# Backward dO projection as column-tile passes, and doubled Q/K row tiles in the forward stage, of a recurrent transformer kernel

One NeuronCore of a Trainium2 chip (trn2) runs the whole program. The metric is device time in microseconds (us) of one execution. Every ratio below is the mean time of one kernel's fast runs over the mean of the other kernel's fast runs of the same rounds, so it is not quite the ratio of the medians that are quoted. Runs were on several chips, and the kernel before took 3682 to 3695 us (medians) on them; compare ratios across groups of runs, not microseconds.

## The reference

```python
for s in range(n_seg):                       # 64 segments of 32 rows, 8 memory rows in front
    h = concatenate([mem, xs], axis=1)       # 40 rows x 512
    q, k, v = (einsum('btd,dhe->bhte', h, W) for W in (Wq, Wk, Wv))   # 32 heads of 128
    p = softmax(where(mask, q @ k.T * scale, -1e9))
    o = einsum('bhte,hed->btd', p @ v, Wo)
    mem = o[:, :M]; outs.append(o[:, M:])    # the memory makes the segments a chain
# around it: layer norm with modulation, a gated linear unit; out: y and all gradients (vjp)
```

In the backward stage the segments run in reverse. For each one dO of every head is `Wo^T dy`. From it come dS, dV, dK, dQ, then `dh`, whose memory rows are the next segment's `dy`.

## The kernel before

The stages run one after the other: forward recurrence, GLU forward and backward, backward recurrence, weight gradients. A scheduler orders each engine's instructions when the program is built; GpSimd (POOL), VectorE (DVE), ScalarE (ACT) and the SP queue then work through theirs in that fixed order.

Backward stage, the projection and what follows it:

```python
rxp = tile_pool(name="p4rx", bufs=3)                    # row buffers for the transposed gradients
def get_dy(s):                                          # dy of a segment by DMA
    nc.sync.dma_start(t[:, :, M:L], self.DAOT[s])
def dot_bank(hb, eng):                                  # WoT stationary, dy (40 columns) moving
    for hh in range(nh):
        for c in range(DC):
            nc.tensor.matmul(ps[:, g_, hl*L:(hl+1)*L], lhsT=WoT[:, c, h*E:(h+1)*E], rhs=dyT[:, c, :], ...)
    self.evac(eng, part3(dOT, hb)[:, :, 0:120], ps[:, :, 0:120])
def grad_part(nm, lh, rh, xt, pi, eng):                 # ... at the end of dVT, dKT, dQT each:
    rows = rxp.tile([128, G, 128], BF16, name="rows_x")
    nc.sync.dma_start(rows[:], xt[:, :], transpose=True)               # SP: transpose, 352 KB
    nc.gpsimd.dma_start({"dVT": self.DVR, "dKT": self.DKR, "dQT": self.DQR}[nm][s], rows[:])   # store
```

Forward stage, what the argument touches:

```python
RA = {x: ptiles("RA" + x, 1, ...)[0] for x in "vkq"}    # one tile of projected rows for v, k, q
def p1_tile(j):                                         # layer norm of 128 rows, some tiles ahead
    x0 = p1w.tile([128, D], BF16, name="x0_1", bufs=1)
    nc.sync.dma_start(x0[:], x_rows[j*128:(j+1)*128, :])
    nc.vector.bn_stats(st[:], x0[:])
    # ... xh, h1 on VectorE, then transposes into hx
```

## Time and profile before

| | us |
|---|---|
| median of 4 runs | 3694.68 (3689.59 to 3696.75) |
| forward recurrence (98 to 1292) | 1194 |
| GLU and its gradients (1292 to 1937) | 645 |
| backward recurrence (1937 to 3044) | 1107 |
| weight gradients (3044 to 3695) | 651 |

In the two recurrences TensorE (PE) is busy over 90% of the time and the other engines feed it; what counts is whatever makes it wait. The prediction shows and reads the lines for this.

### The profile page before, as it was taken

To read this page: it belongs to the slowest core of one execution; us is meant where nothing else is said; L and a number is where in the kernel's file an instruction comes from. 1 tells how busy PE (TensorE), PEld (TensorE's weight loads), DVE (VectorE), ACT (ScalarE), POOL (GpSimd) and SP (SyncE) were. 2 spreads that over 40 slices of the span, in tenths; PEclk is the share of its full clock that TensorE was granted. 3 is DMA by queue.
4 is the path that set the end of the run, shared out by engine and by line. 5 is a ranking of instruction groups with operands and counts; after the bars stand their busy time and mean duration, and the time that the engine had idled before them with its cause. 6 is when DMAs were issued, how large, how long until landed. Compare 5 with 4: busy or idle time off the path is not lost.

```text
span 3696.3 us, 108208 instructions
## 1 busy us (share of the span) xinstructions
PE 3282.3 (89%) x45566; PEld 1897.6 (51%) x45566; DVE 1640.8 (44%) x4087; ACT 1208.9 (33%) x2742; POOL 957.9 (26%) x1917
## 2 busy tenths in 40 slices
PE   1889888899999969996989999999999994999996
PEld 1445444455555535553546666666666662445453
DVE  2454444455545556663225445444455541222222
ACT  0444444444544444442123333333333330000001
POOL 3333333333333323331111112111221221222221
PEclk6999999999999989998999999999999997999998
DMA  7565656566666653324779999999999998787774
GB/s 235 122 134 127 137 131 131 138 137 141 143 139 148 144 163 123 121 102 151 231 213 236 230 228 228 226 223 217 238 246 233 235 212 201 206 207 196 200 197 149
DMA packets 809259, 667.20 MB, mean 181 GB/s; under 512 B 511082, under 2 KB 683898, under 8 KB 808644
## 3 DMA queue, kind: packets, MB, share of 16 engines
q1 hardware_dynamic: 718948, 501.39, 60.5%
q0 software_dynamic: 31024, 103.06, 9.0%
q10 hardware_dynamic: 58800, 55.84, 5.8%
q8 instruction: 357, 5.85, 0.7%
q14 instruction: 130, 1.06, 0.1%
HBM read 292.82 MB, written 275.02 MB: 154 GB/s over the span
## 4 chain that ended last, share of the span: by engine, by line
PE 53%; DMA 5%; issue 3%; DVE 3%; ACT 1%; SPq 1%; POOL 0%; DVEq 0%; ACTq 0%; POOLq 0%
PE gps L1372 11%; PE dh_ps L208 10%; PE proj_ps L1138 6%; PE g_ps L1171 4%; PE gps5o L1382 3%; PE gps L941 3%; PE mm L855 3%; PE dh_tps L208 2%; PE tps L1103 2%; DMA Kst<-KST 2%; PE mm L788 1%; PE mm L792 1%; PE dp_ps L1161 1%; PE dp_ps L1157 1%; PE pass_ps L435 1%
## 5 line engine op out<-in xcount | busy, mean ns | idle before, releaser
L1372 PE MATMUL gps<-rows,hrows 128*128 128x512 bf16 (+2 forms) x2160 | 417.1, 355 | 0.0
L1372 PEld LDWEIGHTS <-hrows 128*128 128x128 bf16 x2160 | 211.4, 98 | 204.2
L647 POOL TENSOR_TENSOR Pst<-Pst,rden 120x1408 bf16<-120x1408 bf16 x64 | 162.7, 2542 | 415.4 <-DMA Pst<-ET 347.3
L1138 PE MATMUL proj_ps<-dyT,WoT 128*128 128x40 bf16 x8192 | 233.1, 180 | 19.4 <-issue 11.8
L1138 PEld LDWEIGHTS <-WoT 128*128 128x128 bf16 x8192 | 223.6, 96 | 30.6 <-issue 30.4
L63 DVE CAST ot<-gps 128x512 bf16<-128x512 f32 (+3 forms) x77 | 48.9, 635 | 395.2 <-PE gps L1372 259.7
L435 PEld LDWEIGHTS <-hT 128*32 128x32 bf16 x6144 | 140.5, 97 | 156.9 <-ACT hT L638 22.4
L234 DVE TENSOR_TENSOR dh_lo<-dh_ps,dh_hi 128x256 bf16<-128x256 f32 x128 | 48.4, 420 | 344.0 <-ACT dh_hi L230 344.0
L1382 PE MATMUL gps5o<-dyrows,rows 128*128 128x512 bf16 x640 | 141.4, 383 | 45.4 <-DMA rows<-OSR 45.4
L61 ACT ACTIVATE ot<-gps 128x512 bf16<-128x512 f32 (+3 forms) x77 | 42.4, 551 | 418.1 <-PE gps L1372 262.5
L208 PE MATMUL at_ps<-Wo,OT 128*32 128x512 bf16 x2048 | 135.0, 384 | 27.9 <-ACT OT L61 25.4
L61 ACT ACTIVATE dVT<-g_ps 128x512 bf16<-128x512 f32 (+1 forms) x192 | 107.8, 561 | 157.3 <-PE g_ps L1171 119.2
L208 PE MATMUL dh_ps<-WvT,dVT 128*32 128x512 bf16 x2048 | 151.8, 391 | 4.6 <-issue 4.5
L1376 POOL DMA_DIRECT2D out_dram<-ot x108 | 81.2, 752 | 281.9 <-DVE ot L63 153.5
L61 ACT ACTIVATE dOT<-proj_ps 128x480 bf16<-128x480 f32 (+2 forms) x192 | 68.4, 391 | 257.8 <-PE proj_ps L1138 250.5
L61 ACT ACTIVATE dQT<-g_ps 128x512 bf16<-128x512 f32 (+1 forms) x192 | 107.8, 561 | 125.1 <-PE g_ps L1171 125.1
L63 DVE CAST dKT<-g_ps 128x512 bf16<-128x512 f32 (+1 forms) x192 | 123.7, 644 | 44.0 <-PE g_ps L1171 43.2
L63 DVE CAST RAq<-pass_ps 128x512 bf16<-128x512 f32 x128 | 88.4, 691 | 121.8 <-PE pass_ps L435 121.8
L234 DVE TENSOR_TENSOR at_lo<-at_ps,at_hi 128x256 bf16<-128x256 f32 x128 | 48.4, 420 | 211.9 <-ACT at_hi L230 211.9
L61 ACT ACTIVATE OT<-tps 128x512 bf16<-128x512 bf16 (+1 forms) x192 | 101.0, 560 | 122.5 <-PE tps L559 91.1
L208 PE MATMUL dh_ps<-WkT,dKT 128*32 128x512 bf16 x2048 | 136.7, 388 | 0.0
L435 PE MATMUL pass_ps<-Wv,hT 128*32 128x512 bf16 x2048 | 126.8, 391 | 9.4 <-ACT hT L638 9.4
(364 smaller groups left out, 7230.7 us busy)
## 6 DMA issues: line engine op xcount, KB each, us to landing
OSR<-Ost SPq DMA_DIRECT2D x64, 352.0 KB
OT<-OT SPq DMA_DIRECT2D x64, 352.0 KB
PS<-Pst SPq DMA_DIRECT2D x64, 352.0 KB
OT_l<-OT SPq DMA_DIRECT2D x64, 352.0 KB
Pst_l<-PS SPq DMA_DIRECT2D x64, 352.0 KB
DVR<-rows_x POOLq DMA_DIRECT2D x64, 352.0 KB, 5.0
DKR<-rows_x POOLq DMA_DIRECT2D x64, 352.0 KB, 6.4
DQR<-rows_x POOLq DMA_DIRECT2D x64, 352.0 KB, 4.7
```

The costliest lines, as they stand in the source:

```text
L61: return nc.scalar.activation(out, in_, AF.Copy)
L63: return nc.vector.tensor_copy(out, in_)
L208: self.nc.tensor.matmul(ps[32 * j:32 * j + 32, :], lhsT=lhsT, rhs=w, start=(n < 4), stop=(n >= total - 4), tile_position=(0, 32 * j))
L234: nc.vector.tensor_tensor(lo[:], ps[:, 256 * h:256 * h + 256], parts[h][:], op=ALU.subtract)
L435: nc.tensor.matmul(ps[32 * j:32 * j + 32, :], lhsT=lhs(c), rhs=rhs, start=(c == 0), stop=(c == DC - 1), tile_position=(0, 32 * j))
L647: nc.gpsimd.tensor_tensor(Pst[0:120, :, :], Pst[0:120, :, :], rden[:, :].unsqueeze(2).to_broadcast([120, G, 128]), op=ALU.mult)
L855: nc.tensor.matmul(hp[:], lhsT=xT[:, fc, :], rhs=wT[:, fc, :], start=(n == 0), stop=(n == 2 * FC - 1))
L941: nc.tensor.matmul(ps[:], lhsT=h2r[:, j, c * 128:(c + 1) * 128], rhs=xr[:, j, :], start=(j == 0), stop=(j == NT - 1))
L1138: nc.tensor.matmul(ps[:, g_, hl * L:(hl + 1) * L], lhsT=WoT[:, c, h * E:(h + 1) * E], rhs=dyT[:, c, :], start=(c == 0), stop=(c == DC - 1))
L1171: nc.tensor.matmul(ps[:, j, :], lhsT=lh[:, g * GW:(g + 1) * GW], rhs=rh[:, g * GW:(g + 1) * GW], start=True, stop=True)
L1372: nc.tensor.matmul(ps[:, 0:ng * E], lhsT=hrows[:, tp_, c * 128:(c + 1) * 128], rhs=rows[:, tp_, 0:ng * E], start=(tp_ == 0), stop=(tp_ == ...
L1382: nc.tensor.matmul(ps[:], lhsT=rows[:, tp_, gg * E:(gg + 1) * E], rhs=dyrows[:, tp_, :], start=(tp_ == 0), stop=(tp_ == NTP - 1))
```

## The change

Intent of the backward part: let WoT be the moving operand, 512 columns at a time, with 32 columns of dy stationary, four column tiles side by side; 32 such matmuls take the place of 128 matmuls of 40 columns. The result lands in rows (RAd) and is turned by 8 transposes. The last 8 rows of each segment ("tails") don't fit into 32; they are projected for four segments together, one tile of four ahead (RBd), turned into `btd`, and copied into dOT by GpSimd. To make room the row buffers go from three to two. Intent of the forward part: K and Q rows in two tiles in turn, so that a store of rows doesn't hold the next segment's rows.

```diff
-            rxp = tile_pool(name="p4rx", bufs=3)
+            rxp = tile_pool(name="p4rx", bufs=2)
+            dOT, RAd, RBd, btd = ...                       # cut
+            def get_da(t):                                 # dy of four segments, one load
+                nc.sync.dma_start(d..., self.DAOT[4*t:4*t+4]...)
+                nc.gpsimd.tensor_copy(b..., d[:, :, :, 24:T])            # dyb, the tails
+            def proj_b(t, hf): self.col_pass(psp, WoT, hf, <dyb>, RBd, ("act", "dve")[hf])
+            def turn_b():
+                for hf in range(2):
+                    tp = self.turn_half(psp, RBd, hf)
+                    self.evac(("act", "dve")[hf], btd[:, 4*hf:4*hf+4, :], tp[:])
-                dot_bank(0, "act"); self.pop_later(); dot_bank(1, "dve"); ...
+                for hf in range(2):
+                    self.col_pass(psp, WoT, hf, lambda c: dyT[:, c, :], RAd, ("act", "dve")[hf])
+                to_heads("pool", btd[:], 0, 8, 32, 8, 8 * s4)          # two copies, btd -> dOT
+                for hf in range(2):
+                    tp = self.turn_half(psp, RAd, hf)
+                    to_heads(("act", "dve")[hf], tp[:], 4 * hf, 4, 0, 32, 0)
+                    prod(hf)
+                if s4 == 0:                                 # end of the body, s4 = s % 4
+                    if s > 0: turn_b()
+                elif s4 < 3 and s > 3: proj_b(s // 4 - 1, 2 - s4)
 # forward
-            RA = {x: ...}
+            RAs = [...]; RA = RAs[s % 2]                    # k and q doubled
-                if norms: norms.pop()()                     # now two steps later
-                outproj(0) ... outproj(1); outproj(2)
+                outproj(0, 6) ... outproj(6, 12) ... outproj(12, 24); outproj(24, H)
# fewer buffers: h1 2 -> 1, hx 5 -> 4, hb 4 -> 3 (cut)
# backward: work of the dh tails in eight pieces and not four; dyT copied by GpSimd out of get_da's tile (cut)
```

## The prediction

> **What bounds the kernel now.** I read the stages first (busy time of each engine in each stretch), then the waits of TensorE in the two recurrent stages, then the chain of work and the timelines of GpSimd and VectorE inside single segments. The change touches two stages: the forward recurrence (98 to 1292 us) and the backward recurrence (1937 to 3044 us), 64 segments each.
>
> ```profile
> 98.00:1292.00 1194.00, 1082.38 (x16922) 596.62 (x16920) 594.92 (x1804) 561.15 (x1468) 390.79 (x1050) 0.97 0.62 137
> 1937.00:3044.00 1107.00, 1047.89 (x21385) 698.12 (x21381) 545.98 (x1332) 347.58 (x795) 222.19 (x461) 0.98 1.07 230
> ```
>
> The columns are stretch, length, then busy time of PE, PEld, DVE, ACT, POOL. PE is busy 95% of the backward stage, so there it is matmul issue time that counts; one segment takes 1107 / 64 = 17.3 us, and one without a stall 16.1 to 16.5 us. The rest is waits:
>
> ```profile
> PE proj_ps L1138 <- issue: 11.8, 8, 2.8
> PE g_ps L1171 <- DMA Kst<-KST: 9.5, 7, 2.5
> ...
> PE dp_ps L1157 <- issue: 5.8, 3, 2.5
> ```
>
> All waits called "issue" in that stage sum to 30.7 us (11.8 + 5.8 + 4.5 + 3.4 + 3.2 + 2.0); in the forward stage they are 0.7 us. What waits there are is this:
>
> ```profile
> PE turn_ps L442 <- DVE RAq L63: 39.9, 8, 5.8
> PE at_ps L208 <- ACT OT L61: 24.3, 50, 0.8
> ...
> 266.66 0.69 DVE L302 BATCH_NORM_STATS2 st<-x 128x6 f32<-128x512 bf16 x1 [7.16 <-DMA x<-in_A_x_dram]
> ```
>
> The first line looks like a full row buffer RAq, which the doubled row tiles would cure. The VectorE timeline shows otherwise: VectorE stands for 7.16 us at the statistics of a later row tile, whose load the SP queue issued late (behind the store of P), and RAq's eviction is the next in its queue. It recurs each 78.6 us. No wait of TensorE or of an eviction for the stores of the K and Q rows shows up.
>
> **What the Trainium skill says.** (1) "TensorEngine Tiling", Key Properties: changing the tiling mode drains TensorE. The trace agrees: from a 128x32 column matmul to a 128x128 one the starts lie 312 ns apart, where the next column group would have followed after 206; back again it is 149 instead of 56 ns. (2) "TensorE: Matmul & The Clock Gate", Part 3, The mechanism: matmuls in different column tiles start about 4 ns apart and run together. The trace has 3 to 4 ns between the four and some 213 ns per group of four. (3) "Advanced Engine Details and Errata", ISA Cache: an instruction line is 16 KB, 256 instructions. The instruction queue moved 167 packets and 2.74 MB in the backward stage, 16.4 KB each, so I read the "issue" stalls as late instruction lines. (4) "DMA: Bandwidth & Descriptors", Issuing engines are not separate DMA queues: transfers from SP and GpSimd interleave on the same 16 engines, so store and transpose times below stretch when loads run beside them.
>
> **The change part by part, backward.** The projection of dO is now 128 matmuls of 40 columns:
>
> ```profile
> 2519.95 1.31 PE proj_ps L1138 x48
> ...
> 2521.32 1.19 PE proj_ps L1138 x48
> ...
> 2523.26 0.80 PE proj_ps L1138 x32
> ```
>
> That is 3.3 us of the path (25 ns apart, 128 x 0.025 = 3.2). After it there are 32 column matmuls, 8 groups x 0.213 = 1.7 us, 8 transposes x 0.056 = 0.45 us, and per four segments the same once more for the tails: (1.7 + 0.45) / 4 = 0.54 us. Bare sum 2.7 us, saving 0.6 us of PE time a segment, or 38 us. But PE work isn't what follows: the result lands in rows and has to be turned. In order, from the start of the passes: last pass matmul 1.5 us, its end 1.9, VectorE eviction (0.69 for 512 columns) 2.6, transposes 2.85, while ACT spreads the first half until 2.95; there the transposes of dOT can begin. VectorE then does the first product (0.42), a copy of 0.2 and the second half's spread (0.5), so its queue frees the second quarter's work at 4.4 us. In the kernel before, the same point (second group of transposes) came at 2524.05 - 2519.95 = 4.1 us. So the body of a segment becomes about 0.3 us longer, although 12 to 24 tail matmuls are now interleaved, because four mode switches (0.1 us each) and the longer evict, turn, spread chain eat the saving: 64 x 0.3 = +19 us.
>
> What is gained: PE instructions fall from 91134 to 81150 rows, and the burst of 256 rows in 3.3 us goes. The issue rate is then like the forward stage's (37 rows a us), which stalls 0.7 us in all: about -25 us. Kst is now loaded ahead of the dQT transpose on the SP queue: about -9 us (its wait).
>
> The expected loss is a new wait on GpSimd. The last 8 rows of each segment come from btd and are copied into dOT by GpSimd. For three segments of four the built program places these copies in the middle of the segment before. For the first of each tile of four (btd has only just been turned) they stand behind the store DQR of the segment before, which itself waits for the DMA transpose of dQT:
>
> ```profile
> 2524.26 0.54 POOL L1177 DMA_DIRECT2D DQR<-rows_x  x1 [3.70 <-DMA rows_x<-dQT]
> ...
> 2507.22 0.54 POOL L1177 DMA_DIRECT2D DQR<-rows_x  x1 [7.82 <-DMA rows_x<-dQT]
> ```
>
> Those are 4.3 and 7.5 us after the start of their segments (2519.95 and 2499.69); over all segments the median is 6.2, the range 3.4 to 10.8 (and the last one). The pool for these rows drops from three buffers to two, so the dQT transpose also waits until DVR has left its buffer (DVR is issued 4.4 to 6.5 us after its transpose and lands about 5 us later), some 1 to 3 us into the next segment; the transpose then lands 4.5 to 5.5 us later. I take 6.5 us. Then 0.54 for the issue and 0.6 for two copies: dOT complete at 7.65 instead of 2.95, a stall of 4.7 us in 15 segments, +70 us. Start of the stage (two passes and a turn of the first tails): +3 us.
>
> **Forward.** The order of instructions on GpSimd and SP in the steady state is the same in both built programs: moving the normalisation in the source doesn't move it. The doubled rows remove no wait that the trace has. Fewer buffers for hx shift one statistics instruction from the crowded start to the steady place, where each costs 5.4 us: +5 us. Splitting the output projection into 6, 6, 12, 8 heads lets ACT evict earlier, but adds two mode switches and one filler matmul ahead of the third part; both ways the last projection matmul starts 2.7 us after the first: 0. The sum: +19 - 25 - 9 + 70 + 3 + 5 = +63 us, 3757 us. I place the centre a little lower, at 3745, because the stall could be shorter where few loads run.
>
> **Rivals.** (a) The projection saving holds. If VectorE's queue is no limit after all and the copies come early (DQR at 4 us), the stall shrinks to 15 x 2.2 = 33 us and the body is 0.3 us shorter: 33 - 19 - 25 - 9 + 8 = -12, about 3680. For it speaks that PE is 95% busy; against it the fixed place of the copies in GpSimd's queue. (b) The two buffers become a ring that binds. A transpose plus a store takes 10 to 12 us of a buffer, three a segment over two buffers make 15 to 18 us, the length of a segment. If latencies don't fall, SP stands still at the transposes, and the loads of Qst and Kst come late in every segment: another 0.5 to 2 us x 64, so 3790 to 3870. Against it: the DMA engines have idle stretches in every segment, and a transpose alone moves its packets in 2 to 3 us. (c) The forward stage gains: if the doubled rows and the earlier evictions take the 5.4 us stalls away, -38 us. I see nothing that would.
>
> **Range and chances.** The stall is 33 to 120 us, the body -19 to +25, stalls removed -34 to -10, the forward stage -15 to +10. Together some 8 times in 10 between 3680 and 3805. Slower by over 2% begins at 3767.6, a little above my sum; faster by over 2% is 3619.9, which needs everything but the stall to turn out twice as well. So 0.03 faster, 0.66 within, 0.31 slower.
>
> **What would show it.** Right: in the waits of TensorE of the backward stage a line of 15 or so waits of 2 to 8 us of the transposes of dOT (or their products) for GpSimd's dOT copies, once per four segments; "issue" in that stage under 10 us; no Kst wait over a few us; the forward stage within 15 us of 1194 with its 5.4 us stalls intact, eight of them. Wrong: no such GpSimd wait (then the copies stood earlier, and the kernel is as fast or faster), waits for Qst, Kst or OT_l in most segments (rival b), or segments without a wait well under 16 us (rival a, my VectorE chain was too long).

## The result and the profile after

The changed kernel takes 3795.2 us (median of 4, 3788.76 to 3812.35); ratio 1.0281 (95% interval 1.0245 to 1.0318): slower. The profiled run, 3810.5 us, is the slowest of the four, so its sums are some 15 us on the large side.

Busy time of each engine in the two stages (columns as in the prediction: stretch, length, PE, PEld, DVE, ACT, POOL, then granted clock, DMA share, GB/s):

```profile
98.00:1296.00 1198.00, 1087.14 (x16906) 632.99 (x16897) 602.82 (x1805) 570.59 (x1470) 393.26 (x1043) 0.97 0.62 136
...
1942.00:3146.00 1204.00, 1068.08 (x16289) 610.37 (x16293) 576.41 (x1486) 372.46 (x821) 271.17 (x662) 0.95 0.90 209
```

The forward stage is 1198 us for 1194. The backward stage is 1204 for 1107, and its granted clock has fallen from 0.98 to 0.95. Waits of TensorE in it (us in total, times, longest):

```profile
PE tps L1150 <- POOL dOT L65: 98.2, 15, 10.1
PE g_ps L1211 <- DMA Qst<-QST: 12.7, 4, 4.5
PE dh_ft L261 <- ACT dh_hi L248: 8.9, 19, 0.5
```

There is the foretold wait, 15 times, once in four segments (in 14 of them the copies stand behind the store DQR; in the first, of 2.1 us, ahead of it). The 30.7 us named "issue" and the 9.5 us for Kst are gone; a wait for Qst is new. One of the 15, on three engines. First GpSimd's timeline, then that of the SP queue (SPq), then TensorE's (start, length, engine, line, instruction; in brackets the idle time before it and what ended it):

```profile
2399.56 0.54 POOL L1217 DMA_DIRECT2D DKR<-rows_x  x1 [4.39 <-DMA rows_x<-dKT]
2405.66 0.54 POOL L1217 DMA_DIRECT2D DQR<-rows_x  x1 [5.56 <-DMA rows_x<-dQT]
2406.20 0.53 POOL L65 COPY dOT<-btd 128x192 bf16<-128x192 bf16 x2
```

```profile
2397.40 0.38 SPq L1156 DMA_DIRECT2D Kst<-KST  x1
2399.34 1.38 SPq L1216 DMA_TRANSPOSE rows_x<-dQT  x1
2407.15 0.39 SPq L1101 DMA_DIRECT2D daq<-DAOT  x1
```

```profile
2398.80 0.39 PE L226 MATMUL turn_ps<-ident,RAd 128*128 128x128 bf16 x4
2406.61 0.50 PE L1150 MATMUL tps<-ident,dOT 128*128 128x128 bf16 x3 [7.43 <-POOL dOT L65]
...
2408.52 0.63 PE L1150 MATMUL tps<-ident,dOT 128*128 128x128 bf16 x4
2408.94 0.63 PE L1197 MATMUL dp_ps<-VT_l,dOT 128*128 128x128 bf16 x4
...
2412.04 0.39 PE L1211 MATMUL g_ps<-Pst_l,dOst 128*128 128x128 bf16 x4
```

The segment starts at 2395.59. The two copies stand in GpSimd's queue behind the store DQR, that store behind the transpose of dQT, and SP issues that transpose only at 2399.34, 1.6 us after the last load before it: it waits for a row buffer. The SP queue's waits in this stage put a name to it:

```profile
SPq L1216 <- DMA DVR<-rows_x: 199.7, 62, 5.1
```

In 62 segments the dQT transpose waited for the dV rows to leave their buffer. TensorE's lines show something the prediction left out: a group of four 128x128 matmuls takes 0.63 us after the stall and 0.39 us from 2412.04 on; the starts lie 0.42 and not 0.23 us apart. For 5.4 us TensorE runs at about half rate. The granted clock of two stretches says the same:

```profile
2393.20:2411.80 18.60, 10.24 (x129) 7.04 (x122) 7.21 (x20) 3.75 (x10) 3.97 (x10) 0.73 0.70 163
2411.80:2428.40 16.60, 16.60 (x263) 8.97 (x261) 7.64 (x22) 5.29 (x12) 2.31 (x5) 0.99 0.93 186
```

The Trainium skill has this in "TensorE: Matmul & The Clock Gate", Part 1: after an idle window of some 3.4 us the clock drops to half, and it comes back after about as long of steady work. The trace agrees: in this stage each of the 16 stalls of 3.4 us or more was followed by a slow stretch, of 2.9 to 6.3 us (TensorE's work at half clock, by the granted-clock records: the trace holds when the clock was granted at half, and the views show the mean). Of the three stalls between 1 and 3 us one was. A stall of 3.4 us isn't needed, though: in the stage of the kernel before (first profile) there is none over 2.9 us, and TensorE worked 33 us of it at half clock.

### The profile page after: what moved, and what is told of

Same layout as the page of the kernel before. It is cut to its first block, busy times and chain, and to the rows that moved or that the text cites. A ratio compares the mean times of both kernels' runs of the same rounds, so it can differ in the third digit from the quotient of the medians.

```text
span 3810.5 us, 98572 instructions
## 1 busy us (share of the span) xinstructions
PE 3311.5 (87%) x40498; PEld 1850.7 (49%) x40574; DVE 1680.1 (44%) x4247; ACT 1245.8 (33%) x2774; POOL 1018.7 (27%) x2128
## 5 line engine op out<-in xcount | busy, mean ns | idle before, releaser
L219 PEld LDWEIGHTS <-hT 128*32 128x32 bf16 x6144 | 163.3, 96 | 127.1 <-ACT hT L649 16.6
L208 PE MATMUL at_ps<-Wo,OT 128*32 128x512 bf16 x2048 | 171.9, 386 | 23.7 <-ACT OT L61 23.7
L1150 PE MATMUL tps<-ident,dOT 128*128 128x128 bf16 x704 | 90.4, 238 | 101.4 <-POOL dOT L65 98.2
L1217 POOL DMA_DIRECT2D DQR<-rows_x x64 | 34.7, 542 | 420.2 <-PE g_ps L1211 182.9
L219 PE MATMUL pass_ps<-Wk,hT 128*32 128x512 bf16 x2048 | 136.5, 383 | 0.0
L219 PE MATMUL pass_ps<-Wq,hT 128*32 128x512 bf16 x2048 | 134.0, 382 | 0.0
L582 DVE TENSOR_TENSOR Ost<-or_ps,rden 120x512 bf16<-120x512 f32 (+1 forms) x192 | 124.2, 647 | 19.2 <-PE or_ps L580 1.1
```

The costliest lines, as they stand in the source:

```text
L208: self.nc.tensor.matmul(ps[32 * j:32 * j + 32, :], lhsT=lhsT, rhs=w, start=(n < 4), stop=(n >= total - 4), tile_position=(0, 32 * j))
L219: self.nc.tensor.matmul(ps[32 * j:32 * j + 32, :], lhsT=lhs(c), rhs=rhs, start=(c == 0), stop=(c == DC - 1), tile_position=(0, 32 * j))
L582: nc.vector.tensor_tensor(part3(Ost, pi)[0:120, 0:n, :], or_ps[0:120, 0:n, :], rden[:, pi * PG:pi * PG + n].unsqueeze(2).to_broadcast([120 ...
L1150: nc.tensor.transpose(ps[:, j, :], src[:, g * w:g * w + GW], self.ident[:, :])
```

## The experiments

Twelve kernels ran, all with correct results, in three groups of four, each group on one chip. The kernel before ran beside each group: medians 3683.0, 3681.8 and 3689.2 us. What was expected of the first four in microseconds starts from the 3694.7 and 3795.2 us of the first measurement; there the ratio counts.

**1. Tails turned earlier (e1_turn_early).**

```diff
                 dstt(0)
+                if s4 == 0 and s > 0:
+                    turn_b()
                 grad_part("dVT", dOst, Pst, dVT, 1, "act")
 ...
                 if s4 == 0:
                     tail.begin(s, [WvT, WkT, WqT])
-                    if s > 0:
-                        turn_b()
```

> The changed kernel with one edit: the eight transposes that turn the tails of the next four segments stand in the middle of the fourth segment and not at its end, so the built program places GpSimd's two copies into dOT in the middle of that segment too, ahead of the transposed row stores. Theory A (the loss is these copies standing behind the store of the dQ rows, plus TensorE running at half rate for some 5 us after each such stall): TensorE's 98 us of waits for GpSimd's dOT copies fall to under 5, the slow stretch after each (18.45 us segments against 16.5) goes as well, about 25 us more, so 3795 - 98 - 25 = 3672, 3660 to 3690. Theory B (the ring of two row buffers is what binds, the copies only show it): TensorE then waits elsewhere, for Qst, Kst or OT_l in most segments, and the time stays above 3740.

Measured: 3754.8 us, ratio 1.0183 (1.015 to 1.0216). Neither theory holds alone. In the built program the copies stand ahead of the store, and the dOT wait is gone, but TensorE now waits here:

```profile
PE g_ps L1211 <- DMA Qst<-QST: 55.7, 21, 6.7
```

and SP's waits for the row buffers have grown in sum (DQR 95.8 and DVR 199.7 us in the changed kernel):

```profile
SPq L1216 <- DMA DQR<-rows_x: 186.7, 45, 9.0
SPq L1216 <- DMA DVR<-rows_x: 152.3, 55, 5.0
```

The stall of one engine had given another its slack. With the copies out of the way the ring of two buffers binds: the SP queue stands at the transposes, and the loads of Qst behind them come late.

**2. Three row buffers (e2_three_row_buffers).**

```diff
-            rxp = tile_pool(name="p4rx", bufs=2)
+            rxp = tile_pool(name="p4rx", bufs=3)
 # room: the fold's hi and lo tiles of the backward stage (names "dh...") with bufs=1 and not 2
```

> The changed kernel with three row buffers again, as before the change (room made by single instead of double buffers for the fold's high and low halves of the backward stage, 2 KB a partition). The copies stay behind the store of the dQ rows. Theory A: the dQ transpose no longer waits for the dV store, so that store is issued some 6 us after the start of a segment and not 8 to 13; each of the 15 stalls shrinks from 6.5 to about 3 us, most of them then too short for the half-rate stretch: 3795 - 15 x 3.5 - 25 x 0.7 - 10 (waits for Qst) = 3715, 3700 to 3735. Theory C (buffers don't matter, only the order on GpSimd): 3785 to 3800.

Measured: 3720.0 us, ratio 1.0093 (1.0054 to 1.0132), as theory A had it. The waits:

```profile
PE tps L1150 <- POOL dOT L65: 42.0, 15, 5.3
```

```profile
SPq L1216 <- DMA DVR<-rows_x: 2.7, 2, 2.2
```

The copies still stand behind DQR, but DQR comes at 5.4 us after the start of those segments on average; in the changed kernel it was 9.7 and in the kernel before 6.4. SP's wait for the dV store has gone from 199.7 to 2.7 us. One more thing moved: in this built program the dQT transpose stands ahead of the loads of Kst, and with two buffers it stood behind them. The third buffer and that place come together, so this run doesn't tell the one from the other; the 199.7 us of SP's waits are the ring's.

**3. The forward part alone (e3_forward_part_alone).** The kernel before with the forward hunks of the diff above.

> The kernel before with the forward part of the change alone (doubled K and Q row tiles, later normalisation, output projection in four pieces, later tail chunk, fewer buffers for the layer-norm tiles). Theory A: the 5 us stalls come from the late load of a row tile and stay, so the forward stage is 1194 to 1200 us as in the changed kernel (1198), and the time is 3694 to 3702. Theory D (the row tiles were the cause of the waits named RAq): 38 us faster, 3656.

Measured: 3687.1 us, ratio 1.0013 (0.9982 to 1.0044). No gain, and the waits that the doubled tiles were meant for are there under their new name (39.9 us in 8 waits before):

```profile
PE turn_ps L226 <- DVE RA0q L63: 41.8, 12, 5.5
```

**4. The backward part alone (e4_backward_part_alone).** The changed kernel with the forward hunks undone.

> The changed kernel with the forward part undone, so the backward part alone. Theory A: all of the loss is here, 3795 - 4 = 3791, 3780 to 3805, with the same 15 waits of TensorE for GpSimd's dOT copies, 90 to 105 us in all. If the two parts interact, it lies outside that.

Measured: 3779.0 us, ratio 1.025 (1.0207 to 1.0292), and 94.9 us of waits for the dOT copies in 14 waits; the time is 1 us under the range that I gave. All of the loss that can be told from noise is in this part.

**5. Both backward edits (e5_early_and_three).** The edits of runs 1 and 2 together.

> The changed kernel with both edits of the two runs before: tails turned early and three row buffers. Each alone left a wait: with early tails alone TensorE waits 55.7 us for Qst (21 times), with three buffers alone 42.0 us for GpSimd's dOT copies (15 times). Theory E (two limits in series, the order on GpSimd and the ring of two row buffers, the second hidden by the first): both waits go, so 3720 (three buffers alone) - 42 - some 20 for the half-rate stretches after those stalls = 3658, 3645 to 3675, and no wait of TensorE in the stage is over 12 us in all. Rival F (with the stalls gone the loads of Qst are late again, because the DMA queues are the bound): waits for Qst of 20 us or more and 3680 to 3700.

Measured: 3687.9 us, ratio 1.0021 (1.0006 to 1.0036). Theory E is right about the waits and wrong about the total. No wait of the stage that counts is left:

```profile
PE dh_ft L261 <- ACT dh_hi L248: 9.6, 20, 0.5
PE dh_ft L261 <- DVE dh_lo L252: 9.2, 17, 0.5
PE pass_ps L219 <- ACT dyT L1281: 8.8, 16, 0.6
```

The stage, from its first pass to its last tail matmul, is 1099.3 us; for the kernel before it was 1114.4 in the first profile and 1099.2 in that of run 6 (whose backward stage is the kernel before's). (The "issue" waits aren't this difference, they are 30.7 and 33.5 us; TensorE worked 33 and 18 us at half clock.) Over all profiles the stage takes 1099 to 1114 us where it is the kernel before's (first profile, runs 3, 6 and 9) and 1099 to 1104 us where it is the mended one (runs 5, 7, 8, 10 and 11). So the mended change shows neither a gain nor a loss in the stage. Compared with run 2 the stretch from the first to the last segment is 41 us shorter, which is the length of the waits; of the 20 us that I had counted for half-rate stretches nothing shows. Undisturbed segments take 16.5 to 16.7 us where they took 16.2 to 16.5 (medians of the distance between the first products with the -1 matrix), and every fourth takes 17.4 or, 8 times in 15, some 18.9. One of the latter in TensorE's timeline: three waits of 0.5 us at its end, one close behind the other, and then a pass of 3.35 us in place of 1.98, so at half rate again. The transposes that run 1 moved away had stood among these waits; that their absence is the reason I take from the timeline, no run tests it.

**6. The load of x placed ahead in the source (e6_before_x_ahead).**

```diff
             nc.sync.dma_start(self.H1ROWS[j*128:(j+1)*128, :], h1[:])
+            if j + 1 < NT:
+                load_x(j + 1)          # p1_tile(j + 1) then uses it
```

> The kernel before, untouched by the change, with one edit in the forward stage: the load of the next row tile of x is issued right after the store of this tile's normalised rows, some 75 us ahead of its use, and not just ahead of its use. Theory A (the 5.5 us stalls of TensorE named RAq are VectorE standing at the statistics of a row tile that SP has loaded late): the seven stalls go (38 us) and the half-rate stretch after each (4.4 to 6 us at half rate, so 2 to 3 us each, 18 in all): 3683 - 56 = 3627, 3615 to 3645. Theory D (the single row tile RAq binds, as the change assumed): no change, 3683.

Measured: 3682.3 us, ratio 1.000 (0.9969 to 1.0031). The theory isn't refuted: the edit did nothing. The two built programs, compared afterwards, have the same instructions in the same order: the scheduler had put the load and the statistics of the next tile right behind the previous tile all along. SP's and VectorE's timelines in this run:

```profile
413.14 0.32 SPq L658 DMA_DIRECT2D PS<-Pst  x1
413.55 1.96 SPq L474 DMA_DIRECT2D QST<-RBq  x3
415.56 1.21 SPq L477 DMA_DIRECT2D QST<-RBq  x2
416.87 0.39 SPq L322 DMA_DIRECT2D H1ROWS<-h  x1
417.36 0.37 SPq L302 DMA_DIRECT2D x<-in_A_x_dram  x1
```

```profile
412.31 0.54 DVE L63 COPY kT<-turn_ps 128x384 bf16<-128x384 bf16 x3
419.54 0.69 DVE L309 BATCH_NORM_STATS2 st<-x 128x6 f32<-128x512 bf16 x1 [6.68 <-DMA x<-in_A_x_dram]
```

VectorE gets to the statistics at some 412.9; SP issues their load at 417.36, because it stood until 413.14 at the store of P and then had six more issues.

**7 and 8. All of these, and the same without the forward part (e7_all_three, e8_all_three_forward_undone).** As run 5 with the edit of run 6; run 8 has the forward hunks undone as well.

> The changed kernel with early tails, three row buffers and the load of x ahead. If the edits add up: 3658 - 56 = 3602, 3585 to 3620, faster than the kernel before by some 2.2%. If the x load is not what stalls, 3658.

> As the run before, but with the forward part of the change undone (single K and Q row tiles, five buffers of hx and so on). Theory A (doubled row tiles and the rest of the forward part are worth nothing, even with the stalls gone): the same within 8 us. Theory D' (they are worth something once the late load is gone): 10 us or more slower.

Measured: ratios 1.0032 (1.0017 to 1.0047) and 1.0006 (0.9989 to 1.0023), medians 3694.8 and 3683.7 us. Since the edit of run 6 does nothing, run 7 repeats run 5. Run 8 says that the backward part with both edits equals the kernel before, and that the forward part costs about 10 us (0.26%) if anything: the two intervals overlap, and run 5, the same built program as run 7, was at 1.0021. Neither theory for run 8 had the forward part cost time.

**9. The load of x on another queue (e9_before_x_on_act).** The kernel before, with

```diff
-            nc.sync.dma_start(x0[:], x_rows[j*128:(j+1)*128, :])
+            nc.scalar.dma_start(x0[:], x_rows[j*128:(j+1)*128, :])
```

> The kernel before with the loads of the row tiles of x issued by ACT's queue instead of SP's. The run that moved this load in the source changed nothing, because the built program had it at the same place already; what delays it is that SP's queue issues it behind seven other transfers, the first of which waits for GpSimd's normalisation of P, some 7 us after VectorE has reached the statistics of that tile. In this built program ACT issues it right after an eviction near the time when the tile's buffer comes free, so VectorE should stand about 1 us. Theory A: the waits of TensorE named RAq fall from some 38 us to under 12, and half-rate stretches after them (2 to 3 us each) go: ratio 0.987, 45 to 50 us less. Theory D (RAq itself binds): ratio 1.00.

Measured: 3628.2 us, ratio 0.985 (0.9825 to 0.9874): faster, and theory A's size. TensorE's wait, VectorE's wait for the row tile (in the kernel before, then in this run), and the stage:

```profile
PE turn_ps L442 <- DVE RAq L63: 9.6, 9, 1.7
```

```profile
DVE st L302 <- DMA x<-in_A_x_dram: 55.8, 9, 8.0
```

```profile
DVE st L302 <- DMA x<-in_A_x_dram: 12.3, 6, 2.9
```

```profile
98.00:1240.00 1142.00, 1062.37 (x16881) 582.26 (x16879) 595.53 (x1796) 559.96 (x1469) 388.00 (x1041) 0.99 0.68 143
```

The wait named RAq went from 39.9 to 9.6 us though RAq is still a single tile. The forward stage went from 1194 to 1142 us and its granted clock from 0.97 to 0.99: 30 of the 52 us are these waits. The other 22 are the half-rate stretches: by the granted-clock records TensorE worked 57 us of the stage at half clock in the kernel before and 12 in this run, and half of the difference is 22. The edit changed more than the load: the scheduler also moved the statistics on VectorE one step ahead (behind the copies of vT and not of kT) and a few small instructions on GpSimd, so the run doesn't tell the earlier load from that step.

**10 and 11. That load with the mended change (e10_backward_mended_x_on_act, e11_all_mended_x_on_act).** Run 10 is the backward part with both edits and the x load on ACT's queue; run 11 has the forward part too.

> The backward part of the change with early tails and three row buffers (forward part undone; ratio 1.0006 when run last), with the load of x on ACT's queue. If the edits add up: ratio 0.988, as the kernel before with that edit alone, so that the mended change is worth nothing either way. If the forward stage's gain doesn't show, 1.00.

> The whole change with early tails, three row buffers and the load of x on ACT's queue. Theory A (the forward part is worth nothing even with the stalls gone, or costs the 5 to 10 us by which it was slower): ratio 0.988 to 0.992. Theory D' (doubled row tiles pay once the late load is gone): under 0.985.

Measured: 0.9863 (0.9842 to 0.9883), 3634.9 us; 0.9881 (0.9858 to 0.9905), 3641.0 us. Both beat both kernels of this study, and neither beats run 9, which has nothing of the change. Doubled row tiles are worth nothing with the stalls gone either; the kernels with the forward part are the slower ones in each pair, by 0.1% (run 3), 0.3% (runs 7 and 8) and 0.2% (runs 11 and 10), but the intervals of each pair overlap.

**12. Control for the room made in run 2 (e12_single_fold_buffers).** The changed kernel with only the fold's tiles single.

> Control for the run with three row buffers: the changed kernel with only the edit that made the room (single instead of double buffers for the fold's high and low halves in the backward stage). They are written once a segment and read within some 2 us, so nothing should wait: as the changed kernel, 15 or so waits for dOT of 90 to 105 us in all, ratio 1.025 to 1.031. If the room-making itself saved or cost time, the run with three buffers has to be read again.

Measured: 3761.2 us, ratio 1.0204 (1.0175 to 1.0233), and not what I expected:

```profile
PE g_ps L1211 <- DMA Qst<-QST: 40.1, 17, 5.8
PE tps L1150 <- POOL dOT L65: 23.7, 9, 5.6
```

The edit had moved instructions: in this built program GpSimd's copies for the first segment of a tile stand just ahead of DQR and not behind it. So it is a second, unplanned case of run 1 (order mended, ring of two left), and it reads the same: dOT waits down, Qst waits up, and most of the loss left (2.0% of 2.8%; in run 1 it was 1.8%). In the built program of run 2 the copies are behind DQR again, which is why its 42.0 us are there; so that run's gain isn't owed to this change of order. What single fold tiles do apart from the order no run shows.

## Why the prediction was wrong in size

The direction and the mechanism were right; the forecast of +50 us was half of the measured +100 (medians). By its own terms, for the two profiled runs (3810.5 - 3696.3 = 114 us; the backward stage from first to last matmul 1114.4 to 1220.0, +105.6):

| term | predicted | measured |
|---|---|---|
| GpSimd's dOT copies behind DQR, 15 times | +70 (15 x 4.7) | +98.2 (15 x 6.5) |
| half-rate stretches | not in the sum | +23 |
| waits for Qst | rival (b) only | +12.7 |
| "issue" waits | -25 | -30.7 |
| Kst wait | -9 | -9.5 |
| body of a segment (+19), start (+3) and rest of the stage | +22 | +12 |
| all before the stage's first matmul (forward part) | +5 | +6 |
| after the stage | 0 | +3 |

The 23 us are half of the slow stretches: by the granted-clock records TensorE worked 78 us at half clock in the changed kernel's stage and 33 in that of the kernel before, mostly behind its "issue" waits. "Body" is the remainder of 105.6.

- **The step that failed is the size of the stall.** The prediction took DQR 6.5 us after a segment's start, near the median of before (6.2). In the segments that matter it came at 9.7 us on average (6.1 to 12.8). I had worked out that the dQT transpose would wait for the dV store, but not by how much the ring shifts it; run 2, with three buffers, put DQR at 5.4 us and the stall at 2.8 (42.0 / 15). An error the other way hid part of this: the transposes of dOT could begin not at 2.95 us but at about 4.2 in these segments (median in run 5, where nothing held them), else the same sum would have given 7.9 us (9.7 + 1.14 - 2.95) and not 6.6.
- **The centre was moved the wrong way.** The prediction's own sum was +63; it went down to +50 because the stall could be shorter. It was longer, in 12 of 15 segments over 4.7 us.
- **The step that was missing is the clock.** A wait was counted at its length. Each one of 3.4 us or more cost 1.4 to 3.1 us on top here (half of the slow stretch), because TensorE then ran at half rate: from a stalled segment's product with the -1 matrix to the next one's it took 18.45 us (median) for 16.5. The page cited in the section on the result says it; the prediction left it out.
- **Rival (b), the ring of two, was not a rival but a second limit behind the first.** In the changed kernel the stalls hide it (12.7 us of Qst waits); in runs 1 and 12 it shows (55.7 and 40.1 us). Only both edits together (run 5) take the loss away.
- **Slips in its working that changed little.** VectorE's steps after the passes add up to 4.1 us (2.95 + 0.42 + 0.2 + 0.5), not 4.4. The second group of transposes came at 4.1 to 4.2 us (medians by place in a tile of four, without the stalled segments) where it had come at 3.9 to 4.1, so that the longer body was partly luck. The forward stage's "37 rows a us" are 28 by the records (16922 + 16920 in 1194 us).
- **Right:** the copies' place and count, the end of the issue stalls with fewer instructions, the Kst wait, the longer body (seen undisturbed in run 5), and that the forward part removes no wait. Its reading of the "issue" waits as late instruction lines is borne out by the trace's DMA records: each of the 25 waits in the first profile ends 1.2 to 1.7 us after a 16 KB packet of the instruction queue has landed, and such a packet comes only each 6.6 us on average. That VectorE's stand at the statistics was what the wait named RAq meant is shown by run 9; it was only argued before.
- **Wrong in the forecast for run 5:** the mended change doesn't gain 24 us on the kernel before, it is even. That the longer segments took what the issue waits gave back is my reading of the segment times; no run tests it.

What stays open: whether in run 2 the third buffer or the earlier place of the transpose did more, and when waits shorter than 3.4 us set off the half rate.

## What to carry to other kernels

Before a copy or a small move is given to an idle engine, look at what stands ahead of it in that engine's queue in the built program: on GpSimd here two copies of 0.5 us in all cost 6.5 us each time, because a store waiting for a transpose stood before them. When one wait is removed, run again with the suspected second limit removed too; alone, the two edits gave back a third and two thirds of the loss, together nearly all. The name of a wait is that of the last hop: a wait for RAq was a load on a busy queue two hops back, and one changed word (another issuing queue, with what the scheduler moved along) was worth 1.5% where doubling the named tile was worth nothing.

## What the Trainium skill lacked or had wrong

- "TensorE: Matmul & The Clock Gate", Part 1: right on the half rate after about 3.4 us of idle. It also has short idles in a row as a cause, but not how short or how many. In the changed kernel's backward stage a stall of 2.06 us was followed by 3.4 us at half clock, two others of 1.52 and 2.75 us were not. In run 5 no stall of the stage after its start is over 1.5 us, and TensorE still worked 30 us of it at half clock.
- "Advanced Engine Details and Errata", ISA Cache: agrees, with 16 KB packets on the instruction queue. It doesn't say what late lines cost: in four profiles of the kernel before's backward stage the waits named "issue" were 28.9 to 34.9 us, and none is listed with 81150 and not 91134 TensorE instructions (matmuls and weight loads) in the built program.
- "DMA: Bandwidth & Descriptors": it has a bandwidth for a DMA transpose, but none that I found for a single one between two SBUF tiles beside other transfers; here one of 352 KB took 6.3 us from issue (2399.34) to the store it released (2405.66).
- No page that I read tells that a buffer count changes the built order on other engines: single fold buffers on ScalarE and VectorE moved two copies ahead of a store on GpSimd, and the waits for them fell from 98.2 to 23.7 us.
